# Loading 64 short rows of W_down: eight transfers of every fourth partition instead of two blocks of 32

## The chip, the cores and the metric

The kernel runs on one core of a Trainium2 chip. The metric is the device time of one execution in microseconds (us), lower is better. Times of several runs are given as a median with the lowest and highest; one further execution was recorded by the hardware profiler, and every row quoted here comes from that recording.

## The reference

One decode step for four sequences (B = 4, one token each, width 512). The normalised input feeds an attention branch over the last 4096 positions of a key/value cache and a gated feed-forward branch; both are added to the input.

```python
def ref(x, k_cache, v_cache, wq, wo, w_gate, w_up, w_down):   # x: [4, 1, 512], bf16
    xn = layernorm(x)
    q = (xn @ wq) as [4, 32 heads, 1, 128]
    k, v = the last 4096 positions of the caches [4, 8, 16384, 128], each of 8 heads used by 4 query heads
    o = softmax(q @ k^T * 128**-0.5) @ v
    attn = o as [4, 1, 4096] @ wo                      # wo [4096, 512]
    ffn  = (silu(xn @ w_gate) * (xn @ w_up)) @ w_down  # w_gate, w_up [512, 1792], w_down [1792, 512]
    return x + attn + ffn
```

About 81 MB have to be read for this: 67 MB of them are the cache window (8 heads, 4 MB of K and 4 MB of V each).

## The kernel before, in words

**The loads.** Nearly all loads are issued by SyncE (`run_sync`) into one DMA queue, in one order that is written out by hand: W_q, W_gate, W_up, then K and V head by head (`load_k`, `load_v`, double-buffered in `KB` and `VB`), then W_down, then W_o, and at the very end the store of the result. A load that reuses a buffer first waits until TensorE has finished with it. Every transfer adds 16 to its semaphore when all of it has landed.

**W_down** has 1792 rows of 512 numbers. 1536 of them (12 on each of 128 partitions, 12 KB a partition) go to `WDA` in one transfer, into the place where W_gate was. The remaining 256 rows (four on each of partitions 0 to 63, 4 KB a partition, 256 KB in all) go to `WDB`, into the place where W_up was. The reason for 64 partitions is the layout of the gate and up products, of which the last group has only 64 columns per tile. Before the change these 64 partitions are loaded in two transfers of 32 partitions. The source is written as eight groups of four rows, but the groups are contiguous, so that the program that is built holds a plain list of 32 rows of 2048 numbers on both sides.

**W_o** (`WO`, 32 KB on each of 128 partitions, in the first K buffer) is loaded in five transfers of 16, 6, 7, 2 and 1 rows of 1 KB a partition (`ROWS`), in that order behind `WDB`, each with a semaphore of its own (`d_wo`).

**TensorE** (`run_tensor`) goes through eight passes of attention (transposes of K at line 417, scores at line 426, values at line 435), and then through the tail `t_tail`: it transposes the attention output, multiplies the feed-forward activations with `WDA` and `WDB` (line 574), waiting for `d_wda` before the first and for `d_wdb` before the thirteenth product, and then multiplies the attention output with the rows of W_o. Rows 0 to 21 are multiplied 512 columns at a time (line 581), waiting for `d_wo[0]` and `d_wo[1]`; VectorE and ScalarE copy that sum out of PSUM (lines 392 and 280); TensorE folds it (line 586) and adds rows 22 to 31 in pieces of 128 columns (line 593), waiting for `d_wo[2]` to `d_wo[4]`. A last cast (line 394) and the store follow.

Of the kernel before, what the change touches and what calls it, by code (L numbers as in the profile page):

```python
# [10 lines left out]
def bass_parallel_sum__sliding_block_cached__swiglu_ffn__decode_kernel(  # L11
# [28 lines left out]
    LAST = HKV  # L40

    TA, TB2, PB = 12, 4, 64
    assert 128 * TA + PB * TB2 == F
    SCALE = float(Dh) ** -0.5
    EPS = 1e-5
# [11 lines left out]
    WDB = WU[:].rearrange("p c n -> p (c n)")[:, 0:TB2 * D].rearrange("p (t n) -> p t n", n=D)  # L57
# [64 lines left out]
    def sem(name):  # L122
        return nc.alloc_semaphore(name=name)
# [7 lines left out]
    d_wdb = sem("d_wdb")  # L131
# [49 lines left out]
    wdb_ap = B_w_down[128 * TA:, :].rearrange("(p t) n -> p t n", t=TB2)  # L181
# [4 lines left out]
    def kv_ap(cache, r):  # L186
        return cache[:, r, Sk - W:, :].rearrange("b (s t) d -> s b (t d)", t=NT)
# [41 lines left out]
    def run_sync(eng):  # L229
        def load_k(r):  # L230
            if r >= 2:
                eng.wait_ge(s_tr[NCH - 1], r - 1)
            eng.dma_start(KB[r % 2][:].rearrange("p t d -> p (t d)"), kv_ap(A_k_cache, r)).then_inc(d_k[r % 2], 16)

        def load_v(r):
            if r:
                eng.wait_ge(s_pv, r)
            eng.dma_start(VB[r % 2][:].rearrange("p t d -> p (t d)"), kv_ap(A_v_cache, r)).then_inc(d_v[r % 2], 16)

        eng.dma_start(WQ[:], wq_ap).then_inc(d_v[1], 16)  # L240
        eng.dma_start(WG[:], wg_ap).then_inc(d_wg, 16)
        eng.dma_start(WU[:], wu_ap).then_inc(d_wu, 16)
        load_k(0)
        load_k(1)
        load_v(0)
        for r in range(2, HKV):
            load_k(r)
            load_v(r - 1)
        load_v(HKV - 1)
        eng.dma_start(WDA, wda_ap).then_inc(d_wda, 16)  # L250

        for u in range(0, PB, 32):
            eng.dma_start(WDB[u:u + 32].rearrange("p t n -> p (t n)"),  # L253
                          wdb_ap[u:u + 32].rearrange("(e p) t n -> e p (t n)", p=4)).then_inc(d_wdb, 16)
        for q, (a, b) in enumerate(ROWS):
            if q == 0:
                eng.wait_ge(s_tr[NCH - 1], HKV - 1)
            eng.dma_start(WO[:, a:b, :], wo_ap[:, a:b, :]).then_inc(d_wo[q], 16)
        eng.wait_ge(s_y, 1)
        eng.dma_start(out_ap, y_ap).then_inc(d_out, 16)  # L260
        eng.wait_ge(d_out, 16)
# [134 lines left out]
    def run_tensor(eng):  # L396
# [6 lines left out]
        def now(reg, lo=1, hi=16 * HKV):  # L403
            return eng.snap(reg, min_val=lo, max_val=hi, donate=True)

        def step(reg, by, op=ALU.add):
            nc.regs_alu(reg, reg, by, op=op)
# [92 lines left out]
        with nc.body("t_a_end", valid_engines=me):  # L500
            j = now(nx, 1, HKV)
# [3 lines left out]
        with nc.body("t_b_end", valid_engines=me):  # L505
            j = now(nx, 1, HKV)
# [3 lines left out]
        with nc.body("t_c_end", valid_engines=me):  # L510
            j = now(nx, 1, HKV)
# [3 lines left out]
        with nc.body("t_values", valid_engines=me):  # L515
            j = now(nx)
# [15 lines left out]
        with nc.body("t_p_end", valid_engines=me):  # L532
            j = now(nx)
# [24 lines left out]
        with nc.body("t_tail", valid_engines=me):  # L558
            eng.wait_ge(s_nm, LAST + 2)
            eng.transpose(rt_ps, OT[:, 1:, :].rearrange("p r c -> p (r c)"), ident[:]).then_inc(s_rt, 1)  # L560
            eng.wait_ge(s_rn, 1)
            for b in range(B):
                for q in range(4):
                    m = mm(op_ps[:, b, :], sel2[:, b, q, :], Rn[:, 32 * q:32 * q + 32],
                           start=(b == 0 and q == 0), stop=(q == 3), skip_group_check=True)
            m.then_inc(s_op, 1)
            eng.wait_ge(s_guT, 1)
            eng.wait_ge(d_wda, 16)
            for t in range(TA + TB2):
                k = (t + 1) % 4  # L570
                if t == TA:
                    eng.wait_ge(d_wdb, 16 * (PB // 32))
                a, w = (guT[:, t, :], WDA[:, t, :]) if t < TA else (guT[0:PB, t, :], WDB[0:PB, t - TA, :])
                mm(part_ps[32 * k:32 * k + 32, :], a, w, start=(t < 3), stop=False, skip_group_check=True)
            eng.wait_ge(s_opc, 1)
            for j in range(EARLY):
                for q, (a, b) in enumerate(ROWS):
                    if a == j:
                        eng.wait_ge(d_wo[q], 16)
                k = (j + 3) % 4  # L580
                m = mm(part_ps[32 * k:32 * k + 32, :], OP[:, j, :], WO[:, j, :], start=False,  # L581
                       stop=(j >= EARLY - 4), skip_group_check=True)
            m.then_inc(s_pt, 1)
            eng.wait_ge(s_ptc, 2)
            for n in range(NC):
                mm(acc_ps[32 * n:32 * n + 32, 0:128], fold[:], part[:, 128 * n:128 * n + 128],
                   start=True, stop=False, skip_group_check=True)
            for j in range(EARLY, 32):
                for q, (a, b) in enumerate(ROWS):
                    if a == j:  # L590
                        eng.wait_ge(d_wo[q], 16)
                for n in range(NC):
                    m = mm(acc_ps[32 * n:32 * n + 32, 0:128], OP[:, j, :], WO[:, j, 128 * n:128 * n + 128],  # L593
                           start=False, stop=(j == 31), skip_group_check=True)
            m.then_inc(s_acc, 1)
            step(seen, 1)
            eng.br_lt(seen, 1, on_true="t_tail", on_false="t_end").branch_hint(loc)
        nc.switch_bb("t_end")

    run_gpsimd(nc.gpsimd)  # L600
    run_sync(nc.sync)
    run_scalar(nc.scalar)
    run_vector(nc.vector)
    run_tensor(nc.tensor)


# [26 lines left out]
```

## Time and profile before

| | us |
|---|---|
| median of 3 runs | 198.91 |
| lowest and highest of them | 198.54 and 199.2 |
| the profiled execution | 198.22 |
| its span, first to last instruction | 197.0 |
| TensorE busy | 155.0 (79%) |
| VectorE busy | 114.6 (58%) |
| ScalarE busy | 68.8 (35%) |

The profiled execution is 0.69 us under the median of the runs; 1.2 us of its time lie outside its span. The page also divides the span in 40 slices of 4.9 us and gives for each the busy share of the engines, the share of its 16 DMA engines that was busy, and the GB/s that these moved. "Granted clock" is the share of TensorE's full clock that the chip allowed in a stretch.

### The profile page before, as it was taken

To read this page: it belongs to the slowest core of one execution; us is meant where nothing else is said; L and a number is where in the kernel's file an instruction comes from. 1 tells how busy PE (TensorE), PEld (TensorE's weight loads), DVE (VectorE), ACT (ScalarE), POOL (GpSimd) and SP (SyncE) were. 2 spreads that over 40 slices of the span, in tenths; PEclk is the share of its full clock that TensorE was granted. 3 is DMA by queue.
4 is the path that set the end of the run, shared out by engine and by line. 5 is a ranking of instruction groups with operands and counts; after the bars stand their busy time and mean duration, and the time that the engine had idled before them with its cause. 6 is when DMAs were issued, how large, how long until landed. Compare 5 with 4: busy or idle time off the path is not lost.

```text
span 197.0 us, 6539 instructions
## 1 busy us (share of the span) xinstructions
PE 155.0 (79%) x2926; PEld 121.2 (62%) x2926; DVE 114.6 (58%) x218; ACT 68.8 (35%) x86; POOL 10.8 (5%) x27
## 2 busy tenths in 40 slices
PE   0038936998998999899899985998599879988444
PEld 0012106986786888689688954885598568755112
DVE  5472373667667586776768664765376756752201
ACT  2003100470563456057246512652156046430001
POOL 8750000000000000000000000000000000000000
PEclk9999975699999999999999999999799999999957
DMA  6999999999999999999999999999999999999991
GB/s 214 439 427 425 472 453 433 416 433 429 423 423 426 426 426 433 426 426 426 426 439 439 433 439 446 439 426 439 426 433 426 426 426 426 433 411 349 370 400 46
DMA packets 3729, 81.09 MB, mean 412 GB/s; under 512 B 456, under 2 KB 588, under 8 KB 1036
## 3 DMA queue, kind: packets, MB, share of 16 engines
q1 hardware_dynamic: 3716, 81.01, 97.0%
q8 instruction: 5, 0.08, 0.2%
q10 hardware_dynamic: 8, 0.00, 0.0%
HBM read 81.01 MB, written 0.00 MB: 411 GB/s over the span
## 4 chain that ended last, share of the span: by engine, by line
DMA 45%; PE 41%; ACT 7%; DVE 3%; SPq 2%; issue 1%; DVEq 0%
DMA kbuf<-in_A_k_cache_dram 29%; PE ps_kt L417 21%; DMA kbuf<-in_A_wo_dram 15%; PE ps_s L426 9%; ACT kT L274 7%; PE ps_o L435 5%; PE ps_s L536 2%; DVE mxb L346 2%; PE ps_s L581 1%; PE ps_kt L523 1%; PE ps_o L540 1%; DVE mx L369 1%; PE ps_s L593 1%; DVE mxd L371 0%; SPq L253 0%
## 5 line engine op out<-in xcount | busy, mean ns | idle before, releaser
L417 PE MATMUL ps_kt<-ident,kbuf 128*128 128x128 bf16 x1024 | 72.3, 227 | 12.0 <-DMA kbuf<-in_A_k_cache_dram 8.5
L417 PEld LDWEIGHTS ps_kt<-ident,kbuf 128*128 128x128 bf16 x1024 | 61.9, 102 | 19.4 <-DMA kbuf<-in_A_k_cache_dram 9.0
L342 DVE COPY kT<-ps_kt 128x1024 bf16<-128x1024 bf16 x80 | 52.2, 687 | 22.8 <-PE ps_kt L417 21.9
L274 ACT COPY kT<-ps_kt 128x1024 bf16<-128x1024 bf16 x48 | 47.8, 1013 | 47.1 <-PE ps_kt L417 47.1
L277 ACT ACTIVATE p<-ps_s 128x512 bf16<-128x512 f32 x32 | 16.5, 603 | 43.5 <-PE ps_s L536 43.5
L346 DVE TENSOR_REDUCE mxb<-ps_s 128x16 f32<-128x512 f32 x32 | 22.1, 692 | 13.2 <-PE ps_s L426 11.6
L426 PE MATMUL ps_s<-qT,kT 128*128 x1024 | 29.4, 169 | 0.0
L426 PEld LDWEIGHTS ps_s<-qT,kT 128*128 128x128 bf16 x1024 | 27.8, 96 | 0.2
L435 PE MATMUL ps_o<-vbuf,p 128*32 128x256 bf16 x576 | 17.4, 273 | 1.3 <-DMA vbuf<-in_A_v_cache_dram 0.7
L435 PEld LDWEIGHTS ps_o<-vbuf,p 128*32 128x32 bf16 x576 | 15.1, 96 | 2.8 <-issue 2.4
L519 PE MATMUL ps_kt<-p,ones 128*128 128x512 bf16 x36 | 9.7, 378 | 0.2
L536 PE MATMUL ps_s<-dsh,lsel 128*128 128x512 bf16 x36 | 9.4, 382 | 0.0
L350 DVE TENSOR_REDUCE dsum<-ps_kt 128x16 f32<-128x512 f32 x9 | 6.2, 692 | 1.5 <-PE ps_kt L519 1.3
L356 DVE TENSOR_TENSOR oT<-ps_o,rden 128x16 f32 (+1 forms) x9 | 1.6, 175 | 8.9 <-PE ps_o L540 8.9
L469 PE MATMUL ps_s<-vbuf,xnT 128*32 128x512 bf16 x32 | 3.6, 629 | 3.6 <-DMA vbuf<-in_A_wq_dram 3.6
L523 PEld LDWEIGHTS ps_kt<-identf,mxd 128*128 128x128 f32 x9 | 1.2, 138 | 8.2 <-DVEq L372 8.2
L581 PE MATMUL ps_s<-kbuf,oP 128*32 128x512 bf16 x22 | 2.8, 623 | 4.4 <-DMA kbuf<-in_A_wo_dram 4.4
L523 PE MATMUL ps_kt<-identf,mxd 128*128 128x128 f32 x9 | 2.9, 322 | 4.3 <-DVEq L372 4.3
L540 PEld LDWEIGHTS ps_o<-fold,o 128*128 128x128 f32 x36 | 5.4, 190 | 1.3
L280 ACT COPY part<-ps_s 64x512 f32<-64x512 f32 x1 | 0.6, 580 | 14.8 <-PE ps_s L581 14.8
L459 PE MATMUL ps_s<-ident,xn 4*128 4x4 bf16 x4 | 0.3, 166 | 6.9 <-DVE xn L305 6.9
L392 DVE COPY part<-ps_s 64x512 f32<-64x512 f32 x1 | 0.7, 683 | 8.1 <-PE ps_s L581 8.1
(92 smaller groups left out, 77.9 us busy)
## 6 DMA issues: line engine op xcount, KB each, us to landing
kbuf<-in_A_k_cache_dram SPq DMA_DIRECT2D x8, 4096.0 KB, 26.9
vbuf<-in_A_v_cache_dram SPq DMA_DIRECT2D x8, 4096.0 KB, 28.8
vbuf<-in_A_wq_dram SPq DMA_DIRECT2D x1, 4096.0 KB, 12.3
kbuf<-in_A_wo_dram SPq DMA_DIRECT2D x1, 2048.0 KB, 30.4
wg_sb<-in_B_w_gate_dram SPq DMA_DIRECT2D x1, 1792.0 KB, 16.2
wu_sb<-in_B_w_up_dram SPq DMA_DIRECT2D x1, 1792.0 KB, 20.0
wg_sb<-in_B_w_down_dram SPq DMA_DIRECT2D x1, 1536.0 KB, 26.1
kbuf<-in_A_wo_dram SPq DMA_DIRECT2D x1, 896.0 KB, 33.5
```

Of the source, the lines that this page charges most:

```text
L274: eng.copy(KT[n % 8][:], kt_ps[n % 3]).then_inc(s_ev[n], 1)
L277: eng.activation(P[:, q * TB:(q + 1) * TB, :], S_ps[q], ACT.Exp, scale=SCALE).then_inc(s_xp[q], 1)
L342: eng.tensor_copy(KT[n % 8][:], kt_ps[n % 3]).then_inc(s_ev[n], 1)
L346: eng.tensor_reduce(mxb[:, q, :], S_ps[q].rearrange("p t c -> p c t"), AX.X, ALU.max)
L350: eng.tensor_reduce(dsum[:], dn_ps[:].rearrange("p (t c) -> p c t", c=CQ), AX.X, ALU.add)
L417: last = eng.transpose(kt_ps[n % 3][:, k, :], KB[g][:, 8 * n + k, :], ident[:])
L426: last = mm(S_ps[q][:, 8 * (n % 4) + k, :], KT[n % 8][:, k, :], QT[:, bass.ds(j, 1), :, :].rearrange("p o b h -> p (o b h)"), start=(n % 4 ...
L435: last = mm(o4_ps[32 * k:32 * k + 32, :], P[:, 2 * u:2 * u + 2, :].rearrange("p t c -> p (t c)"), VB[e][:, 2 * u:2 * u + 2, :].rearrange(" ...
L519: last = mm(dn_ps[:], ones[:], P[:, q * TB:(q + 1) * TB, :].rearrange("p t c -> p (t c)"), start=(q == 0), stop=(q == NB - 1))
L523: eng.transpose(mx_ps, mxd[:], identf[:]).then_inc(s_mt, 1)
L536: mm(S_ps[q], Lsel[:], bc(Dsh[:], TB), start=False, stop=True, skip_group_check=True).then_inc(s_sh[q], 1)
L540: last = mm(ot_ps, o4[:, 128 * e:128 * e + 128], fold[:, 16 * e:16 * e + 16], start=(e == 0), stop=(e == 1), skip_group_check=True)
```

## The change

The transfers of `WDB` are cut differently. Before, transfer u took partitions u to u+31 (u = 0, 32). Now there are eight transfers; the one that starts at partition u = 32a + j (a = 0, 1; j = 0 to 3) takes the eight partitions u, u+4, ..., u+28, with the same 4 KB for each. The same bytes go to the same places. TensorE's wait before the thirteenth feed-forward product asks for 8 x 16 increments instead of 2 x 16. Nothing else is touched.

```diff
     TA, TB2, PB = 12, 4, 64
+    WDB_FIRST = [32 * u + j for u in range(PB // 32) for j in range(4)]
...
         eng.dma_start(WDA, wda_ap).then_inc(d_wda, 16)
 
-        for u in range(0, PB, 32):
-            eng.dma_start(WDB[u:u + 32].rearrange("p t n -> p (t n)"),
-                          wdb_ap[u:u + 32].rearrange("(e p) t n -> e p (t n)", p=4)).then_inc(d_wdb, 16)
+        for u in WDB_FIRST:
+            eng.dma_start(WDB[u:u + 29:4], wdb_ap[u:u + 29:4]).then_inc(d_wdb, 16)
         for q, (a, b) in enumerate(ROWS):
...
                 if t == TA:
-                    eng.wait_ge(d_wdb, 16 * (PB // 32))
+                    eng.wait_ge(d_wdb, 16 * len(WDB_FIRST))
```

## The prediction

> **What bounds the kernel now.** I read the page's slices first, then the chain that ended last, then the stretch around the W_down loads.
>
> ```profile
> PE   0038936998998999899899985998599879988444
> DMA  6999999999999999999999999999999999999991
> GB/s 214 439 427 425 472 453 433 416 433 429 423 423 426 426 426 433 426 426 426 426 439 439 433 439 446 439 426 439 426 433 426 426 426 426 433 411 349 370 400 46
> ```
>
> The DMA engines are busy in every slice from the second to the last but one, TensorE is not. The bytes move at about 426 GB/s, with one dent: slices 37 to 39 (349, 370, 400), about 177 to 192 us. The end of the chain of waits, in order of time (start, length, what):
>
> ```profile
> 156.91 0.54 SPq L238
> ...
> 158.12 0.43 SPq L253
> 158.55 0.05 issue
> 158.60 0.42 SPq L253
> 159.02 0.04 issue
> 159.06 30.39 DMA kbuf<-in_A_wo_dram
> 189.45 0.14 issue
> 189.59 2.84 PE ps_s L581 x22
> ...
> 192.45 0.69 DVE part L392
> ...
> 193.19 0.66 PE ps_s L586 x8
> 193.84 1.00 PE ps_s L593 x40
> ...
> 194.86 0.29 DVE y_sb L394
> ```
>
> Everything behind 189.45 waits for W_o, which stands last in the load queue. Whatever delays that queue in its last 30 us delays the end by as much. Line 253, the WDB transfers, is the piece in front of it. Its neighbourhood (columns: stretch, length, then busy time and instructions of PE, PEld, DVE, ACT, POOL, granted clock, DMA share, GB/s):
>
> ```profile
> 165.00:175.00 10.00, 8.91 (x222) 7.58 (x219) 7.02 (x15) 3.95 (x4) 0.00 (x0) 1.00 0.98 423
> ...
> 180.00:181.00 1.00, 1.00 (x36) 0.71 (x26) 0.07 (x1) 0.00 (x0) 0.00 (x0) 1.00 1.41 352
> 181.00:182.00 1.00, 1.00 (x8) 0.69 (x6) 0.35 (x1) 0.00 (x0) 0.00 (x0) 1.00 0.74 193
> 182.00:183.00 1.00, 0.71 (x4) 0.29 (x3) 0.40 (x2) 0.00 (x0) 0.00 (x0) 1.00 1.20 418
> 183.00:184.00 1.00, 0.80 (x22) 0.63 (x26) 0.37 (x1) 0.00 (x0) 0.00 (x0) 1.00 0.95 258
> 184.00:185.00 1.00, 0.83 (x16) 0.20 (x8) 0.36 (x1) 0.00 (x0) 0.00 (x0) 1.00 0.89 360
> 180.00:185.00 5.00, 4.34 (x77) 2.53 (x66) 1.56 (x4) 0.00 (x0) 0.00 (x0) 1.00 1.04 316
> 185.00:190.00 5.00, 0.57 (x12) 0.20 (x12) 0.00 (x0) 0.00 (x0) 0.00 (x0) 0.77 0.98 408
> ```
>
> From 180 to 185 us the engines are as busy as ever (share 1.04) but move 316 GB/s instead of 423: packets take longer. Missing are (423 - 316) x 5 us = 535 KB, or 1.26 us of the whole queue, around a load of 262 KB. That is the stall the change can touch.
>
> **How it lies on the path.** Time from issue to landing of the last V, of WDA, and of the first part of W_o (its 30.39 us stand in the chain above):
>
> ```profile
> L238 SPq DMA_DIRECT2D vbuf<-in_A_v_cache_dram x1: 535/535/535, 156.9 to 156.9; - x1
> ...
> DMA to landing us min/median/max: 21.9/21.9/21.9
> ...
> L250 SPq DMA_DIRECT2D wg_sb<-in_B_w_down_dram x1: 592/592/592, 157.5 to 157.5; - x1
> ...
> DMA to landing us min/median/max: 26.1/26.1/26.1
> ```
>
> V lands at 156.91 + 21.9 = 178.81, WDA at 157.49 + 26.1 = 183.59, W_o's first part at 189.45. A DMA engine moves 423/16 = 26.4 GB/s. Between the first and the last of these moments it carries 96 KB of WDA (3.72 us), its share of WDB, and 128 KB of W_o (4.96 us). Without WDB that is 8.69 us; it took 189.45 - 178.81 = 10.64. So WDB costs the path 1.95 us now, of which its own bytes, 16 KB for each of 16 engines, are 0.62 and the stall 1.33 (the sum over the queue gave 1.26). WDA alone took 4.78 instead of 3.72: the latest engines were slowed before they had a byte of WDB to carry, by other engines' WDB. So it is something shared that stalls, not the carrying of 4 KB pieces.
>
> **How many engines carry it.** From the page:
>
> ```profile
> DMA packets 3729, 81.09 MB, mean 412 GB/s; under 512 B 456, under 2 KB 588, under 8 KB 1036
> q1 hardware_dynamic: 3716, 81.01, 97.0%
> q10 hardware_dynamic: 8, 0.00, 0.0%
> ```
>
> The 456 smallest packets are 16 pieces of the store, and else completion increments. The load of x (q10, 4 partitions) has 4 pieces and 4 completions, so a transfer of four rows ends on four engines; the store, four rows wide on one side, I take alike. 25 transfers of 128 partitions on 16 engines make 400. 456 - 16 - 400 - 4 - 4 = 32 are left for two WDB transfers: 16 engines each, two partitions an engine. After the change a transfer has eight rows, so by the row of x it ends on eight engines, and each of these carries one row of each of the eight transfers: 32 KB on eight engines, nothing on the other eight.
>
> **The change part by part.** (1) The bytes. For the eight carrying engines 32,768 B / 26.4 = 1.24 us in place of 0.62, for the other eight 0 in place of 0.62. (2) The stall. [...] If a group of partitions takes in no more than its share of 423 GB/s, 64 partitions take 211 GB/s, and 262 KB need 1.24 us at the least, however cut; the 1.95 of now are that plus collisions. [...] The trace before shows no load of this cut, so the stall left is bounded by the rows: 0 (as between 165 and 175 us) to 1.33 (all of it). [...] Gain: 1.95 - 1.24 = 0.71 us. With the slower row behind the dent as the measure (408 GB/s, 25.5 an engine) the other loads take 9.00 of the 10.64, WDB 1.64 now and 1.28 then, and the gain is 0.36.
>
> [...]
>
> (3) Six more transfers. On SP each issue takes 0.43 + 0.04 us by the chain (158.12 to 158.60), so W_o is issued 6 x 0.47 = 2.8 us later, at 161.9 instead of 159.06. V, in front of it in the same queue, lands at 178.81: 17 us of cover, and I cost it at nothing; if the cover were gone it would be the 2.8. On the queue, by the two last parts of W_o:
>
> ```profile
> L258 SPq DMA_DIRECT2D kbuf<-in_A_wo_dram x5: 423/432/432, 159.1 to 160.9; - x5
> ...
> kbuf<-in_A_wo_dram SPq DMA_DIRECT2D x1, 256.0 KB, 33.7
> ...
> kbuf<-in_A_wo_dram SPq DMA_DIRECT2D x1, 128.0 KB, 33.6
> ```
>
> They are issued some 0.47 apart and land 0.37 apart, where 131 KB / 423 = 0.31: 0.06 for eight short pieces and a completion on each engine. Six times that, 0.36, is the upper end, 0 the lower; I take a ninth, one packet of nine, 0.04.
>
> [...]
>
> (4) The waits. TensorE's wait for `d_wdb` asks for 128. Behind it are four WDB products and all of W_o's; the four are done at 185.16, and then TensorE idles 4.42 us for W_o:
>
> ```profile
> 184.76 0.40 PE L574 MATMUL ps_s<-wu_sb,guT 64*32 64x512 bf16 x4 [0.17 <-DMA wu_sb<-in_B_w_down_dram]
> 189.59 2.82 PE L581 MATMUL ps_s<-kbuf,oP 128*32 128x512 bf16 x22 [4.42 <-DMA kbuf<-in_A_wo_dram]
> ```
>
> WDB should land near 178.81 + 3.72 + 1.24 = 183.8, so this costs nothing. (5) The tail. All five parts of W_o move alike. The last lands about 160.9 + 33.6 = 194.5, and TensorE ends 194.84, so it follows the loads even though it has half its clock there (0.50 from 188 us); it keeps its length.
>
> Sum: -0.71 + 0.04 = -0.67 us. On the profiled execution that is 198.22 - 0.67 = 197.55, and on the median, which stands 0.69 higher, 198.91 - 0.67 = 198.24.
>
> **The rivals.** (a) Slower: the stall is bound to reading or writing these 4 KB rows, whoever carries them, and stays at 1.33. Then eight engines pay 1.24 + 1.33 = 2.57 for 1.95, and with 0.04 the time is 199.57. For it: the trace cannot tell the reading end from the writing end. Against it: WDA's last packets, longer pieces, stall too, and the stretch 181 to 182 is at its worst when most rows have been sent. It decides once more than 0.67 us of stall is left. (b) The late engines are not among the eight. At the end only a few engines are still loading:
>
> ```profile
> 192.00:193.00 1.00, 0.40 (x2) 0.00 (x0) 0.55 (x1) 0.55 (x1) 0.00 (x0) 0.50 0.35 134
> 193.00:193.50 0.50, 0.31 (x8) 0.20 (x8) 0.13 (x1) 0.03 (x1) 0.00 (x0) 0.50 0.28 104
> ```
>
> 104 / 26.4 = 4 of 16, more than 1 us behind the others, and these set every landing. If all four are in the idle half, the path saves the whole 1.95: 197.0. If they lay anyhow, (1/2)^4 = 0.06. With some of them there the gain lies between. (c) No change: the rows are still spread over 16 engines, or the collisions move to the late engines and half of the stall (0.67) stays: 198.9. (d) Each of the six extra transfers costs a fixed 0.11 us: six eat the 0.71, and the time is 198.9. The 0.06 of the last part of W_o speaks against it, and I count it with (c). [...]
>
> **How the numbers follow.** Forecast 0.58, with its own range 197.8 to 198.6 (a late engine or two outside the eight; the 408 baseline with dear completions); (a) 0.13; (b) 0.09, over the 0.06 because nothing says the late ones are placed at random; (c) and (d) 0.20. What a measurement of this kernel tells from no change is about 0.3%, 0.6 us, so the forecast lies just beyond it: I put three quarters of its chance to faster. Faster 0.43 + 0.09 + 0.01 = 0.53, same 0.15 + 0.18 = 0.33, slower 0.13 + 0.01 = 0.14. The range runs from (b), 197.0, to a stall of which nearly all is left, 199.5.
>
> **What will show it.** In the profile after: the queue q1 with 3716 + 32 = 3748 packets and 488 under 512 B (64 completions); with 16 engines still at work more. GB/s from 180 to 185 near 400 and no second at 193 or 258. WDA's time to landing 1.07 shorter, 25.0; W_o's first part landing near 188.8. The forecast is wrong if the dent keeps its depth, if W_o lands later than 189.45, or if the last loading is done by more than a few engines.

## The result and the profile after

The changed kernel takes 197.23 us (median of 15 runs, 196.03 to 198.27) against 198.62 for the kernel before (15 runs, 198.24 to 199.2): a ratio of 0.9919, 95% interval 0.9895 to 0.9942, so 0.8% or some 1.4 us faster, twice the 0.67 us of the forecast and in its direction. It lies within the range as a whole (197.0 to 199.5), but below the forecast's own 197.8 to 198.6 and close to the 197.0 of rival (b). The profiled execution has a span of 195.9 us against 197.0. (Its own time is 198.16: in some executions of the changed kernel, and of most others here, some 2 us instead of 1.2 lie outside the span. So I compare spans below where single executions are meant.) The ratios leave out executions over 1.5% above the fastest of their kernel, two of e4 and three of e11, which the medians and spans below include.

The slices of the page, in the order of those of before:

```profile
PE   0028935997998999899899985998799849987643
DMA  6999999999999999999999999999999999999991
GB/s 222 435 423 430 471 455 428 425 425 422 425 425 422 435 442 435 428 428 435 428 435 428 428 428 428 428 428 428 428 428 428 428 435 428 428 429 409 434 371 37
```

Where 349, 370 and 400 stood there are now 409, 434 and 371; the last falls because engines run out of work (DMA share 0.77 from 190.0 us and 0.60 from 190.4), not because they stall (the pieces of W_o take at most 0.62 us for 16 KB and 0.25 for 6 KB there). The stretches around the WDB load (stretch, length, busy time and instructions of PE, PEld, DVE, ACT, POOL, granted clock, DMA share, GB/s):

```profile
165.00:175.00 10.00, 8.85 (x218) 7.43 (x217) 6.99 (x16) 3.82 (x4) 0.00 (x0) 1.00 0.98 423
...
180.00:181.00 1.00, 1.00 (x29) 0.60 (x19) 0.28 (x1) 0.00 (x0) 0.00 (x0) 1.00 1.02 418
181.00:182.00 1.00, 1.00 (x8) 0.77 (x6) 0.15 (x1) 0.00 (x0) 0.00 (x0) 1.00 1.20 504
182.00:183.00 1.00, 0.68 (x9) 0.30 (x10) 0.40 (x2) 0.00 (x0) 0.00 (x0) 1.00 0.89 373
183.00:184.00 1.00, 1.00 (x28) 0.50 (x24) 0.58 (x1) 0.00 (x0) 0.00 (x0) 1.00 1.04 442
...
180.00:185.00 5.00, 4.15 (x69) 2.27 (x58) 1.55 (x4) 0.00 (x0) 0.00 (x0) 1.00 1.03 433
```

316 GB/s have become 433: the dent is gone, and the microseconds of 193 and 258 GB/s with it. The trace shows the same packet by packet: the 4 KB pieces of WDB took 0.16 to 0.39 us each before and 0.16 each now, and the late 12 KB pieces of WDA, 0.46 us elsewhere, took up to 1.37 before and 0.46 now. The queues, and the end of the chain of waits:

```profile
DMA packets 3761, 81.08 MB, mean 414 GB/s; under 512 B 489, under 2 KB 621, under 8 KB 1069
q1 hardware_dynamic: 3748, 81.01, 96.8%
```

```profile
155.34 0.54 SPq L239
155.88 0.04 issue
155.92 0.59 SPq L251
156.51 0.04 issue
156.56 0.78 SPq L254
157.34 0.05 issue
157.39 0.68 SPq L254
...
161.43 0.62 SPq L254
162.06 0.04 issue
162.10 0.44 SPq L258
...
164.01 29.46 DMA kbuf<-in_A_wo_dram
193.47 0.04 issue
193.51 0.27 PE ps_s L593 x4
193.78 0.02 issue
193.81 0.29 DVE y_sb L394
```

3748 packets on q1 are the 32 more that eight engines a transfer should give. The last part of W_o lands at 193.47 instead of 194.5, and the span is shorter by about as much (1.1). TensorE is back at full clock here at the end, and the tail behind the last landing is as short as before (0.31 us to TensorE's end, in both).

The gain is not one number. Of the 21 runs of the changed kernel that I have (15, and 6 in e1), 15 have spans of 195.6 to 196.1 us and 6 of 194.8 to 195.1, with nothing between. The kernel before has one group, from 196.9 to 198.0.

### The profile page after: what moved, and what is told of

It reads as the page before. It is cut to its first block, busy times and chain, and to the rows that moved or that the text cites. A ratio compares the mean times of both kernels' runs of the same rounds, so it can differ in the third digit from the quotient of the medians.

```text
span 195.9 us, 6536 instructions
## 1 busy us (share of the span) xinstructions
PE 152.4 (78%) x2917; PEld 118.8 (61%) x2926; DVE 114.4 (58%) x218; ACT 68.8 (35%) x86; POOL 10.8 (6%) x27
## 3 DMA queue, kind: packets, MB, share of 16 engines
q1 hardware_dynamic: 3748, 81.01, 96.8%
## 4 chain that ended last, share of the span: by engine, by line
DMA 44%; PE 37%; ACT 7%; SPq 5%; DVE 3%; issue 2%; DVEq 0%
DMA kbuf<-in_A_k_cache_dram 29%; PE ps_kt L417 20%; DMA kbuf<-in_A_wo_dram 15%; PE ps_s L426 9%; ACT kT L274 7%; PE ps_o L435 5%; SPq L254 3%; PE ps_s L536 2%; DVE mxb L346 2%; SPq L258 1%; PE ps_kt L523 1%; PE ps_o L540 1%; DVE mx L369 1%; DVE mxd L371 0%; SPq L243 0%
## 5 line engine op out<-in xcount | busy, mean ns | idle before, releaser
L417 PE MATMUL ps_kt<-ident,kbuf 128*128 128x128 bf16 x1024 | 70.9, 224 | 12.6 <-DMA kbuf<-in_A_k_cache_dram 9.0
L417 PEld LDWEIGHTS ps_kt<-ident,kbuf 128*128 128x128 bf16 x1024 | 60.2, 100 | 20.4 <-DMA kbuf<-in_A_k_cache_dram 9.5
L346 DVE TENSOR_REDUCE mxb<-ps_s 128x16 f32<-128x512 f32 x32 | 22.1, 692 | 13.2 <-PE ps_s L426 11.6
L519 PE MATMUL ps_kt<-p,ones 128*128 128x512 bf16 x27 | 7.6, 379 | 0.9 <-ACT p L277 0.2
L354 DVE COPY o<-ps_o 128x256 f32<-128x256 f32 x9 | 3.8, 425 | 2.5 <-PE ps_o L435 1.9
## 6 DMA issues: line engine op xcount, KB each, us to landing
kbuf<-in_A_wo_dram SPq DMA_DIRECT2D x1, 2048.0 KB, 26.3
wg_sb<-in_B_w_down_dram SPq DMA_DIRECT2D x1, 1536.0 KB, 26.4
```

The source lines that it names most:

```text
L346: eng.tensor_reduce(mxb[:, q, :], S_ps[q].rearrange("p t c -> p c t"), AX.X, ALU.max)
L417: last = eng.transpose(kt_ps[n % 3][:, k, :], KB[g][:, 8 * n + k, :], ident[:])
L519: last = mm(dn_ps[:], ones[:], P[:, q * TB:(q + 1) * TB, :].rearrange("p t c -> p (t c)"), start=(q == 0), stop=(q == NB - 1))
```

## The experiments

Each was compared with the kernel before on the same chip (its medians there: 198.64 for e1 to e4, 198.81 for e5 to e8, 198.62 for e9 to e11). Spans are those of all runs. Where these fall in two groups, the median stands in one of them and the ratio weighs both. The last column is the stretch 180 to 185 us of the profiled execution.

| | median us | ratio, 95% interval | spans us (runs) | GB/s |
|---|---|---|---|---|
| before | 198.62 | 1 | 196.9 to 198.0 | 316 |
| after | 197.23 | 0.9919 [0.9895, 0.9942] | 194.8-195.0 (5), 195.6-196.1 (10) | 433 |
| e1 after again | 197.16 | 0.9918 [0.9889, 0.9948] | 195.1 (1), 195.8-196.0 (5) | 432 |
| e2 eight neighbours | 197.14 | 0.9938 [0.9908, 0.9969] | 195.5-195.9 (8), 197.2-198.2 (4) | 300 |
| e3 source blocks | 197.13 | 0.9909 [0.9881, 0.9938] | 194.7 (1), 195.8-196.4 (5) | 425 |
| e4 upper half | 199.45 | 0.9998 [0.9965, 1.0030] | 195.9-196.2 (4), 197.9-198.5 (8) | 253 |
| e5 no WDB load | 196.09 | 0.9863 [0.9837, 0.9889] | 194.7-194.9 (4) | 426 |
| e6 before, WDB twice | 201.22 | 1.0112 [1.0089, 1.0136] | 199.6-200.2 (5) | 203 |
| e7 after, WDB twice | 198.46 | 0.9960 [0.9936, 0.9985] | 195.8-196.1 (4), 197.1-197.4 (8) | 430 |
| e8 128 partitions | 196.87 | 0.9908 [0.9885, 0.9932] | 195.4-195.7 (6) | 434 |
| e9 one load | 196.78 | 0.9898 [0.9874, 0.9923] | 195.4-195.7 (6) | 435 |
| e10 two halves | 198.18 | 0.9972 [0.9955, 0.9989] | 196.5-197.3 (12) | 325 |
| e11 upper half again | 199.57 | 0.9997 [0.9962, 1.0033] | 196.0-196.3 (4), 198.2-198.6 (8) | 253 |

**What the load costs: e5, e6, e7.** e5 leaves the load of WDB out; the four products stay and read W_up's leftovers.

```diff
-        for u in WDB_FIRST:
-            eng.dma_start(WDB[u:u + 29:4], wdb_ap[u:u + 29:4]).then_inc(d_wdb, 16)
...
-                if t == TA:
-                    eng.wait_ge(d_wdb, 16 * len(WDB_FIRST))
```

> The load of WDB is left out (the four products stay and read what W_up left there). It measures the whole price of WDB before the change and after it. From the profile before, 10.64 us between the last V's landing and W_o's first less 8.69 for the other bytes: 1.95 us less than before, near 196.7. If only the 535 KB missing in the dent counted (1.26 us of stall, 0.62 of bytes): 1.88 less. If the load was hidden anyway: as before, 198.6.

```profile
159.58 32.67 DMA kbuf<-in_A_wo_dram
192.26 0.04 issue
```

W_o's last part lands at 192.26, so in the profiled executions the load cost 194.5 - 192.26 = 2.2 us before and 193.47 - 192.26 = 1.21 after. By medians it cost 2.72 before (198.81 less 196.09). The spans of e5 lie within 0.2 us, those of the kernel before within 1.1, so the stall differs from execution to execution. The 1.95 was too little; the 1.24 for eight engines carrying 32 KB each was right. e6 and e7 load WDB a second time into a free place, in the old cut and in the new one (shown is e7; e6 repeats the two transfers of 32; the wait asks for both copies):

```diff
+    WDC = WU[:].rearrange("p c n -> p (c n)")[:, TB2 * D:2 * TB2 * D].rearrange("p (t n) -> p t n", n=D)
...
+        for u in WDB_FIRST:
+            eng.dma_start(WDC[u:u + 29:4], wdb_ap[u:u + 29:4]).then_inc(d_wdb, 16)
```

> The kernel before, with WDB's two transfers of 32 partitions issued a second time into a free part of W_up's place. By the stall theory each pair costs the queue its bytes and the stall again: 1.95 us more, 200.5. If the stall belongs to the change from one load to the next and not to the bytes: only the 0.62 of its bytes, 199.2.

> The changed kernel, with its eight transfers issued a second time into a free part of W_up's place. If a set costs the eight carrying engines 32 KB each and nothing else, 1.24 us more where a late engine is among the eight, less where none is: about 198.3, under 200.5 of the doubled kernel before. If eight extra issues of 0.66 us on SP, or their fixed cost in the queue, begin to show: above 199.

The old cut pays 2.4 us for a second copy (201.22 against 198.81), again more than 1.95, so the stall goes with the bytes. The stretches of e6, from 165, 180 and 185 us:

```profile
165.00:175.00 10.00, 8.85 (x222) 7.56 (x220) 7.12 (x15) 3.95 (x4) 0.00 (x0) 1.00 0.99 426
180.00:185.00 5.00, 3.31 (x62) 2.19 (x50) 1.53 (x4) 0.00 (x0) 0.00 (x0) 1.00 1.10 203
185.00:190.00 5.00, 2.09 (x16) 0.45 (x16) 0.00 (x0) 0.00 (x0) 0.00 (x0) 0.50 0.95 330
```

The dent is deeper and longer. The new cut shows none with twice the load (430 GB/s), and the middles of its two groups of spans stand 1.3 us apart: over the 194.8 of e5 they lie near 1.2 and 2.5, where the single load has them near 0.1 and 1.1.

**What stalls: e2, e3, e4 and e11, e8, e10.** e3 keeps the partitions that are written and reads blocks of eight consecutive rows, so W_down's last rows are permuted (i counts the transfers).

```diff
-        for u in WDB_FIRST:
-            eng.dma_start(WDB[u:u + 29:4], wdb_ap[u:u + 29:4]).then_inc(d_wdb, 16)
+        for i, u in enumerate(WDB_FIRST):
+            eng.dma_start(WDB[u:u + 29:4], wdb_ap[8 * i:8 * i + 8]).then_inc(d_wdb, 16)
```

> As the change on the side that is written (every fourth partition), but each transfer reads eight consecutive rows of the source. This permutes W_down's last 256 rows among the partitions, so the feed-forward products of these rows are other ones; amount and order of the work are the same. Theory P (the written side decides): as the changed kernel, 197.2, no dent in the GB/s. Theory H (it was the reads that collided, and rows 16 KB apart avoid it): the dent comes back in part or in full, 198.0 to 199.5.

```profile
165.00:175.00 10.00, 8.98 (x210) 7.95 (x208) 7.03 (x12) 4.96 (x5) 0.00 (x0) 0.98 0.99 426
180.00:185.00 5.00, 4.68 (x96) 3.31 (x98) 1.83 (x6) 0.00 (x0) 0.00 (x0) 1.00 1.01 425
```

As the changed kernel, without a dent: the spacing of the rows that are read changes nothing here (425 GB/s against 433, 197.13 us against 197.23). The other side is what counts. e4 writes the same eight-row transfers to partitions 64 to 127:

```diff
+            eng.dma_start(WDB[64 + u:64 + u + 29:4], wdb_ap[u:u + 29:4]).then_inc(d_wdb, 16)
```

> The change's transfers, but written to partitions 64 to 127 (64 + u, 64 + u + 4 and so on); the products still read partitions 0 to 63, where W_up's numbers are left, so WDB's part of the sum is another one. Same source, same eight engines, same cut. Theory P, with engines 0 to 7 normally writing partitions 0 to 63 and engines 8 to 15 the others: now the eight carriers write where the other eight are writing W_down and W_o, the stall is back, 198.3 to 199.5. Theory R, or a theory in which only the spacing of the partitions counts: as the changed kernel, 197.2.

```profile
165.00:175.00 10.00, 8.85 (x215) 7.66 (x217) 6.51 (x13) 4.96 (x5) 0.00 (x0) 1.00 0.98 423
180.00:185.00 5.00, 4.15 (x86) 2.89 (x78) 1.91 (x6) 0.00 (x0) 0.00 (x0) 1.00 1.09 253
```

Moving the target by 64 partitions, with cut and source unchanged, brings the dent back, deeper than before the change (253 against 316 GB/s), and 8 of 12 runs lose all of the gain. So it is not the eight-row transfers as such, nor the step of four, but which partitions they write into. The cleanest pair has the same bytes for each of 128 partitions. e8 lays the last 256 rows out as two on each of 128 partitions (the main lines, against the kernel before):

```diff
-    TA, TB2, PB = 12, 4, 64
+    TA, TB2, PB = 12, 2, 128
...
-        for u in range(0, PB, 32):
...
+        eng.dma_start(WDB, wdb_ap).then_inc(d_wdb, 16)
```

e10 is e8 with this load in two transfers, of partitions 0 to 63 and 64 to 127:

```diff
-        eng.dma_start(WDB, wdb_ap).then_inc(d_wdb, 16)
+        for u in range(0, PB, 64):
+            eng.dma_start(WDB[u:u + 64], wdb_ap[u:u + 64]).then_inc(d_wdb, 16)
```

> W_down's last 256 rows as two on each of 128 partitions (2 KB a partition) in one transfer, instead of four on each of 64; the gate and up products of these columns are laid out as two tiles of 128 columns instead of four of 64, and two products instead of four use them. The result is the reference's. [...] Theory P: no stall, price 0.62 plus some 0.05 for shorter pieces instead of 1.95: 1.3 us less than before, 197.3, and by theory L with one group of spans (no engine carries more than another). If 2 KB pieces stall too: 198.0 or more.

> As the cut with two rows on each of 128 partitions, but in two transfers, partitions 0 to 63 and 64 to 127. Sixteen engines again carry four pieces of 2 KB in each, the same bytes for every engine, no wrong half left out; the result is the reference's. [...] Theory P (the stall comes from engines writing where others write): it is back, 198.0 to 199.5, with a dent in the GB/s from 180 to 185. Theory S (the stall had to do with 4 KB pieces or with 64 partitions holding more bytes than the rest): as the single transfer, 196.9.

Stretches from 165 and 180 us of e8, and then of e10:

```profile
165.00:175.00 10.00, 8.85 (x217) 7.41 (x216) 6.91 (x15) 3.76 (x4) 0.00 (x0) 1.00 0.98 423
180.00:185.00 5.00, 3.98 (x64) 2.23 (x55) 1.55 (x4) 0.00 (x0) 0.00 (x0) 1.00 1.04 434
```

```profile
165.00:175.00 10.00, 8.92 (x215) 7.63 (x215) 6.46 (x13) 4.83 (x5) 0.00 (x0) 1.00 0.98 419
180.00:185.00 5.00, 4.55 (x84) 2.73 (x72) 1.77 (x5) 0.00 (x0) 0.00 (x0) 1.00 1.05 325
```

One cut in two, 434 GB/s against 325, and spans of 195.4-195.7 against 196.5-197.3 with no overlap. The load sent into one half of the partitions at a time stalled the queue; sent over all 128 it did not. That is what theory P said; theory S is out, since e10 has 2 KB pieces and an even load on all partitions, and stalls.

e4 fits theory P only under that theory's own assumption on which engines write which half; no run here shows which engine writes where. That engines which carry nothing of the load slow down too is shown by e2, next.

e2 shows the limit of the simple picture. It takes eight consecutive partitions at a time:

```diff
-    WDB_FIRST = [32 * u + j for u in range(PB // 32) for j in range(4)]
+    WDB_FIRST = range(0, PB, 8)
...
+            eng.dma_start(WDB[u:u + 8], wdb_ap[u:u + 8]).then_inc(d_wdb, 16)
```

> Eight transfers of eight partitions as in the change, but consecutive ones (u to u+7) instead of every fourth. [...] Theory P (what stalls is several engines writing into the same small group of partitions): the stall is back and larger than before the change, up to 8 x 0.62 = 5 us for the whole load instead of 1.24, time 199 to 202. Theory R (what mattered is that eight engines carry instead of sixteen, wherever they write): as the changed kernel, 197.2.

My 199 to 202 was a miss: 8 of 12 runs lie where the longer group of the changed kernel lies (195.5 to 195.9), only 4 are slower (197.2 to 198.2), and none reaches its shorter group (194.8 to 195.1). The profiled one is of the slower kind:

```profile
165.00:175.00 10.00, 8.85 (x217) 7.66 (x218) 6.68 (x14) 4.68 (x5) 0.00 (x0) 1.00 0.98 423
180.00:185.00 5.00, 4.10 (x74) 2.42 (x62) 1.55 (x4) 0.00 (x0) 0.00 (x0) 1.00 1.04 300
```

In this trace the engines without WDB, which go straight on to W_o from 180.0 us, are slowed as well: their 16 KB pieces take up to 1.03 us up to 182, against 0.62 in the changed kernel. I had taken the eight engines to stall one another in every execution; why 8 of 12 runs were short was not shown. e11 repeated e4 for the same question:

> The transfers to partitions 64 to 127 once more; the products read what W_up left in partitions 0 to 63, as before. Its 12 runs had two groups, spans of 195.9 to 196.2 (4) and 197.9 to 198.5 (8). Theory G (whether the queue stalls depends on where the late engines lie in that execution): both groups come again at about 1 to 2, and a profile of the short kind shows no dent from 180 to 185 us, one of the long kind a dent like the 253 GB/s of the first. Theory N (the short ones were single accidents): nearly all 197.9 to 198.5.

Both groups came again, 4 and 8 of 12, so the short ones are no accidents. Its profile was of the long kind once more (253 GB/s). What an execution of e4 must have to be short stays open: no profile of a short one was caught. It need not have escaped the stall. None of the 24 runs of e4 and e11 reaches the 194.8 to 195.1 of the changed kernel's shorter group, so the short ones may as well be stalled executions in which the late engines, of which more below, carry no WDB.

**The two groups of the changed kernel: e1 and e9.**

> The changed kernel once more, unchanged, beside the others. Its 15 runs fell in two groups of spans, 194.8 to 195.0 us (5 runs) and 195.6 to 196.1 (10). Theory L (the late engines lie among the eight that carry WDB in some executions and outside in others): both groups come again, about 1.1 us apart, and a profile of the shorter kind shows the last part of W_o landing with no late engine that carried WDB. Theory M (a mere effect of the clock in the tail): the spans spread evenly. Median 197.2 on both.

Both groups came again, the shorter with one run, 0.7 us apart at the nearest. The profile is of the longer kind, so the shorter was not seen in a trace. What the trace of the longer shows is how the engines finish (changed kernel, stretches as above):

```profile
190.40:191.00 0.60, 0.60 (x9) 0.06 (x6) 0.00 (x0) 0.00 (x0) 0.00 (x0) 0.50 0.60 232
191.60:192.20 0.60, 0.05 (x4) 0.06 (x8) 0.49 (x1) 0.39 (x1) 0.00 (x0) 1.00 0.17 63
192.20:192.80 0.60, 0.60 (x32) 0.41 (x36) 0.00 (x0) 0.00 (x0) 0.00 (x0) 1.00 0.13 46
```

232 GB/s are nine engines' worth (at 26.4 each), 46 fewer than two: the engines finish in steps, and the last microsecond belongs to about two that are both late and carriers. Before, four were left. The trace also records the sixteen landings of a transfer on sixteen engines one by one (the sixteen increments of a semaphore do not come at once). In every trace here four of them come about 1 us after the other twelve, already for the V of 157 us (changed kernel: twelve by 157.85, four from 158.92). W_o's first part lands on twelve engines by 185.9 and on four from 187.0 in e5, and in the changed kernel on six by 185.9, on eight from 186.5 to 187.2, and on two at 188.4. So two of the four late engines carried WDB in this execution, and in e1's, which has the same steps; both belong to the longer group. The clock is no rival for the 1.1 us: in e1's trace it is still halved at the end, and TensorE ends 0.2 later (193.96 against 193.78) with the last landing 0.1 later. e7 fits: a second set moves the long group by 1.3 us and the short one by 1.1, the price of 32 KB on a carrier, in the short group because carriers that were on time have become the last. Theory L explains all of this; that in the shorter executions no late engine carries WDB, so that the late engines change place from run to run, is argued from the groups, not seen. e9 takes away the unequal share: all of W_down as 14 rows on each of 128 partitions, in one transfer.

```diff
-    TA, TB2, PB = 12, 4, 64
+    TA = F // 128
...
-    wda_ap = B_w_down[0:128 * TA, :].rearrange("(p t) n -> p t n", t=TA)
-    wdb_ap = B_w_down[128 * TA:, :].rearrange("(p t) n -> p t n", t=TB2)
+    wda_ap = B_w_down.rearrange("(p t) n -> p t n", t=TA)
...
-                        v = wb[:, c] if k == 3 else wa[:, c, 4 * k:4 * k + 4, :]
+                        v = wa[:, c, 4 * k:min(4 * k + 4, TA), :]
```

> W_down as 14 rows on each of 128 partitions in a single transfer of 14 KB pieces; the separate load of the last 256 rows, its semaphore and its wait are gone, and the result is the reference's. [...] Price over the kernel without that load (span 194.8): 16 KB / 26.4 = 0.62 us, span 195.4, time 196.7, one group of spans, a little under the transfer of 2 KB pieces (195.6). If the fifteen more strided columns of the gate and up products slow TensorE early on, nothing changes, since the queue sets the end. If merging does not help beyond the other cut: 196.9.

```profile
180.00:185.00 5.00, 4.04 (x68) 2.29 (x56) 1.55 (x4) 0.00 (x0) 0.00 (x0) 1.00 1.02 435
```

196.78, one group of spans (195.4 to 195.7), 0.6 to 0.9 over the 194.8 of e5: the price of 16 KB on every engine. It has the best median of all that load the whole of W_down, and one transfer and one wait fewer than e8. Against the changed kernel the difference of 0.4 us is inside the intervals, and that kernel's shortest runs (196.03) are shorter. What e9 and e8 show is one group of spans each, in six runs: with equal shares no second group appeared.

## Why the prediction came out as it did

**The place and the mechanism held.** The dent from 180 to 185 us was the cost, it lay on the path, and it went (433 GB/s). WDB landed at 183.9 where 183.8 was foretold; the queue had 3748 packets on q1, as worked out (and 489 small ones for 488).

**What the load cost before: too small.** The 1.95 us of the step "How it lies on the path" measure 2.2 in the profiles and 2.72 by medians (e5); the stall in them is not 1.33 but 1.6 and 2.1. Two things were off, a small one and a large one. The last V, from which I counted, landed at 178.81 here and at 156.5 + 22.1 = 178.6 without the load. These 0.2 us are in the 2.2 and not in the 1.95, and they are not the load's: the first piece of WDB started at 180.0, after V. So the sum for this one execution was nearly right.

```profile
L239 SPq DMA_DIRECT2D vbuf<-in_A_v_cache_dram x1: 535/535/535, 156.5 to 156.5; - x1
...
DMA to landing us min/median/max: 22.1/22.1/22.1
```

The large one: the profiled execution was one of the shortest of its kernel, a span of 197.0 where the runs reach 198.0, and the forecast carried its stall over to the median as if every run had the same. With the price by medians before and the 1.21 of the trace after, the sum is -2.72 + 1.21 = -1.5, near the measured -1.4. Besides, the median of 198.91 from which the forecast subtracted was that of three runs; fifteen gave 198.62, so 0.3 of the 1.0 us between 198.24 and 197.23 is the starting point. That the median lies near the 197.0 of rival (b) is partly luck: most runs pay the 1.2 that (b) does away with.

**Own bytes of the eight engines: right.** 1.24 foretold, 1.21 measured. **Stall left: right**, none (each 4 KB piece took 0.16 us). The 0 was an estimate, the lower of the two bounds. That the written partitions decide is borne out by e4, e8 and e10 (253, 434 and 325 GB/s); which engine writes which was not seen. The limit for a group of partitions, which led to the same 1.24, was an estimate that no run shows.

**Late engines, rival (b): the other term that was mis-sized.** That four are late was right. I took it as one case with 0.09 that holds for the kernel or doesn't. By the groups it comes and goes by execution: 6 of 21 runs pay next to nothing for WDB (194.8 to 195.1, as e5). (1/2)^4 supposed that each late engine falls anywhere by itself; 6 of 21 suggests that they come together. Its 197.0 also came out at 196.0 to 196.3, by the same too small 1.95.

**Rival (a)**, the stall stays with the rows whoever carries them, is excluded: no dent, and e3 clears the reading side. **Rivals (c) and (d)**: sixteen engines it was not, and the eight transfers cost 1.21 together with their bytes, so no fixed cost shows. The 0.06 of term (3) came from landings rounded to tenths; recorded to hundredths they are 194.20 and 194.53, 0.33 apart, which leaves 0.02.

**Six more issues on SP: dearer than said, and hidden as said.** A transfer of every fourth partition takes SP 0.62 to 0.78 us (rows of line 254 above), not 0.43. It is not the eight engines: e2's transfers, eight neighbours each and as many packets in all (3748 on q1), take 0.28 to 0.38.

```profile
L254 SPq DMA_DIRECT2D wu_sb<-in_B_w_down_dram x8: 278/295/381, 156.6 to 159.1; - x8
```

So in the changed kernel W_o was issued 5.6 us after WDA's issue ended (156.51 to 162.10) instead of 1.0: 4.6 later, not 2.8. V's landing still covers it.

**The marks.** "WDA's time to landing 25.0" was badly chosen: it shows 26.4, and yet WDA landed at 155.92 + 26.4 = 182.3, 1.3 earlier than before. The time to landing did not shrink, because the issue itself had come 1.6 earlier. Landing times count from the issue; compare the moments. W_o's first part landed at 162.10 + 26.3 = 188.4; 188.8 was foretold.

```profile
kbuf<-in_A_wo_dram SPq DMA_DIRECT2D x1, 2048.0 KB, 26.3
...
wg_sb<-in_B_w_down_dram SPq DMA_DIRECT2D x1, 1536.0 KB, 26.4
```

## What to carry to other kernels

Where a queue of loads sets the end, look for stretches in which the DMA share stays at 1 and the GB/s fall: there packets take longer (here a share of 1.04 at 316 GB/s, and 4 KB pieces of up to 0.39 us against 0.16), and the transfer in that place is worth cutting anew. Let every transfer write all 128 partitions at once where the layout allows (it did here, at 434 and 435 GB/s in e8 and e9, and e9 saved a transfer); else try eight rows, every fourth of 32. That cut worked into partitions 0 to 63 (433 GB/s); into 64 to 127 (253) it lost the gain in 16 of 24 runs. A price read from one profiled execution is that execution's; if single runs fall in groups, forecast the groups.

## What the runs showed that was not expected

Sixteen engines that wrote into partitions 0 to 63 alone slowed the whole queue (193 GB/s in the worst microsecond before), and so did eight-row transfers into partitions 64 to 127 (253 over five in e4); in e2 engines that carried none of these rows were slowed too (16 KB pieces of up to 1.03 us against 0.62). Issue of a transfer of every fourth partition cost SP 0.62 us or more, against 0.43 for 32 consecutive ones and some 0.30 for eight. And the changed kernel, whose engines carry unequal shares, fell in two groups of times, 1.1 us apart.
